# Four-chunk Strassen scheme of a sparse-attention and MLP kernel: DMA issues behind the exponentials, new shares of down steps, a pair's first block moved

## The chip, the core and the metric

The kernel runs on one core of one Trainium2 chip. The metric is the device time of one execution in microseconds (us), median of several runs. The program is written with a fixed schedule: the order in which the Python code issues instructions is the order in which each engine runs them. TensorE is PE in the rows, its weight loads PEld, VectorE DVE, ScalarE ACT, GpSimd POOL, SyncE SP; a q behind the name (ACTq, SPq) marks the engine's sequencer at work, as when it issues a DMA.

## The reference

Block-sparse attention over 4 x 8 heads of 768 x 64, then an MLP on its 3072 x 512 output.

```python
mask = np.abs(blk_i - blk_j) <= 1            # blocks of 32
mask |= (blk_i == 0) | (blk_j == 0) | (blk_i == 23) | (blk_j == 23)
for qb in range(24):
    for kb in sampled_blocks[qb]:            # three more key blocks
        mask[qb*32:(qb+1)*32, kb*32:(kb+1)*32] = True
scores = np.where(mask, scale * q @ k.T, -1e9)
attn = softmax(scores)
x = (attn @ v).transpose(0, 2, 1, 3).reshape(3072, 512)
h = x @ w_in                                 # 512 x 2048
g = h * (1.0 / (1.0 + np.exp(-1.702 * h)))
out = g @ w_out                              # 2048 x 512
```

## The kernel before

**The MLP.** The 3072 tokens are six chunks of 512, the 2048 hidden features sixteen slices of 128. A step m is one slice of one chunk: `up` makes h (12 matmuls of 128x512), `gate` makes g by a tanh on ACT and a product on DVE (`times`, L610 or L986), and `down` adds g times a slice of w_out to four output banks (12 matmuls). Every fp32 factor is split in a high and a low part, so a product is three matmuls. `gate_hi` casts g to ghi on ACT (L615), `gate_lo` subtracts on DVE (L623). `down` is two parts: 8 matmuls with ghi (L650, L652), then 4 with glo (L646).

**w_out.** Its rows stand in DRAM as `ws`; `stream` (L573) fetches the 256 KB of one slice into a tile `wst`, `split` casts the high part on ACT (L578) and subtracts the low part on DVE (L579) into one of three `wout` tiles. In the first chunk the weights are converted from 64-bit words instead (`weights`: L501, L516 on ACT, L540 to L551 and L509 on DVE).

**Attention.** An item is 64 query rows of all heads: `scores` (L343, 32 matmuls into banks 0 and 1), `least` (maximum on DVE, L360, and its negation nm, L362), four exponentials on ACT (L378), transposes of the exponentials (`turned`, L396, four to a bank, copied out by ACT, L402), `values` (L425, 64 matmuls), `normalise` (DVE, L441 to L451), and `turn` (L458, two transposes), whose result ACT and DVE split into x (L465, L466).

**The stages.** Chunks 0 and 1 run as 32 ticks (`tick`), with the attention items set among the quarters of the ticks by `plan`: an item begins every three quarters. Chunks 2 to 5 run in `last`: twice, eight calls of `pair(p)` do the up steps of two chunks by a seven-product Strassen scheme, in blocks of 6 matmuls (`half`, L970). A pair starts with block a11 x b11 into bank x, which ACT copies out (`snap`, L1001) before the block s2 x t2 is added to the same bank. One chunk of the two goes down within the pass, in `slot`s; the gates of the other are kept. Between the two passes stands `stretch`: the 16 down steps of the kept chunk (`drain`, a generator that yields after each matmul) run among the last 16 attention items. `go(k)` takes k of these 192 matmuls.

In `stretch`, item j is issued in this order: scores of item j, `least`, values of item j-2, transposes of item j-1, `go(DRAIN)`, exponentials of item j, `turn` of item j-2, first transposes of item j. A down step sets three lists of work for other engines, `hooks`: [0] casts, [1] subtractions, [2] the next `stream`, on ACT's queue. At the start of each down step `drain` calls `settle()`, which empties all three, so a `stream` that falls due in `go` stands ahead of the exponentials on ACT:

```python
least()
...
self.settle((1,))
go(DRAIN if g else 4)
finish(exps)
```

The tile into which a `stream` writes is that of the slice just split, so the DMA waits for the subtraction L579 on DVE. DMAs of SP and ACT also take eight completion semaphores in turn, and each waits for the one eight before it.

Of the kernel before, what the change touches and what calls it, by code (L numbers as in the profile page):

```python
# [27 lines left out]
NF = DF // P  # L28
# [3 lines left out]
CT = CU * UT  # L32
# [10 lines left out]
MAIN = (NC - TAIL) * NF  # L43
LATE = 2 * CU
NEXTQ = QT * NF - 4
STRIDE = 3
DRAIN = 10
SPARE = (7, 1, 2, 0)
DV = D + 1
VROW = H * DV  # L50
# [7 lines left out]
class Kernel:  # L58
# [640 lines left out]
    def plan(self):  # L699

        at = {}
        assert all(self.sparse(g) for g in self.behind + self.latter)
        starts = [(8 * k - 8 if k < CU else NEXTQ + STRIDE * (k - CU), g) for k, g in enumerate(self.behind)]
        starts.append((starts[-1][0] + STRIDE, None))
        put = lambda q, part, g: at.setdefault(q, []).append((part, g))
        for k, (q, g) in enumerate(starts):
            before = starts[k - 1][1] if k else None
            turn = q + (2 if k >= CU else 4)
            if g is not None:
                if q >= 0:  # L710
                    put(q, self.scores, g)
                if turn >= 0:
                    put(turn, self.transposes, g)
            if before is not None:
                assert q >= 0
                put(q, self.values, before)
                put(turn, self.turn, before)
        return at
# [9 lines left out]
    def tick(self, m):  # L728

        n0, n1, n2 = 0, 0, 0  # L730
# [4 lines left out]
        def run(n):  # L735
            for _ in range(n):
                next(self.conv, None)
# [17 lines left out]
        put_off, self.put_off = self.put_off, None  # L755
        self.up(m, range(2, 4))
        after = self.begin(QT * m + 2)
        soon = NF - 3 <= m < NF
        self.gate(m, lambda: (self.flush(), run(0 if soon else n1)))
        if soon:  # L760
            run(n1)
        finish(put_off)
        finish(after[:3])
        self.down(m - LAG, 0)
# [220 lines left out]
    def times(self, g, h):  # L985
        self.nc.vector.scalar_tensor_tensor(out=g, in0=g, scalar=1.0, in1=h, op0=ALU.add, op1=ALU.mult)  # L986

    def pair(self, p):

        nc = self.nc  # L990
        x, z, y = (self.bank[SPARE[n]] for n in (p % 2, 2, 3))
        a11, a12, a22 = self.block(2 * p + 1, 0), self.block(2 * p + 1, 1), self.block(2 * p, 1)
        s1, s2, s3, s4 = ([w[:, n] for w in self.sums] for n in range(4))
        b11, b21, b22, t1, t2, t3, t4 = self.right
        again = self.again
        m = MAIN + 2 * NF * again + 2 * p

        def snap(bank):
            s = self.store2[:, CT * (4 + self.nsnap % 4):CT * (5 + self.nsnap % 4)]
            self.nsnap += 1  # L1000
            nc.scalar.copy(out=s, in_=bank)  # L1001
            return s

        two = p or again
        self.half(x, a11, b11, True)
        p1 = snap(x)
        self.half(z, a12, b21, True)
        self.add(p1, p1, z)
        self.room_for(p)
        self.slot(m - 2 if two else m - 1, 0)  # L1010
        next(self.prep, None)
# [33 lines left out]
            self.mixed(p + 1)  # L1045
        if not again and p == 0:
            self.keep_sums(1)
        g = self.work.tile([P, CT], F32, name="g")
        self.tanh(g, u2)
        self.times(g, u2)  # L1050
# [2 lines left out]
            self.slot(m - 1, 1)  # L1053
        self.tanh(self.kept(2 * p), x)
        self.times(self.kept(2 * p), x)
        self.gate_hi(m + 1)
        self.gate_lo(m + 1)

    def kept(self, f):

# [54 lines left out]
    def drain(self, start, end):  # L1115

        for d in range(start, end):
            self.settle()
            if d + 1 >= start + 2:
                self.next_gate(d + 1)  # L1120
            for part in range(2):
                yield from self.products(d, part)
            self.split(d + 2, self.hooks)
            if d + 6 < end + 4:
                self.hooks[1].append(lambda d=d: self.hooks[2].append(
                    lambda: self.stream(d + 6, ("wst", "g")[(d + 6) // 2 % 2], self.nc.scalar)))

    def stretch(self):
# [5 lines left out]
        def go(k):  # L1134
            for _ in range(k):
                next(todo, None)

        items = self.latter
        self.hooks = [], [], []
        self.where = {"s": (0, 1), "t": (2, 2), "a": (7,)}  # L1140
        start, end = MAIN + NF - 2, MAIN + 2 * NF - 2
        todo = self.drain(start, end)
# [9 lines left out]
        self.settle()  # L1152
        self.room(1, tr, self.store2)
        self.klimit, self.vlimit = len(self.kent), len(self.vent)
        go(16)
        self.settle()
        prep = self.prepare_again()
        n = len(items)
        for j in range(n + 2):
            g, one, two = (items[k] if 0 <= k < n else None for k in (j, j - 1, j - 2))  # L1160
            exps = []
# [8 lines left out]
            if one:  # L1170
                self.turned(one, 1)()
            self.settle((1,))
            go(DRAIN if g else 4)
            finish(exps)
            if two:
                finish(self.turn(two))
# [6 lines left out]
            self.settle((0,))  # L1183
            if j in (11, 13, 14, 15, 16, 17):
                next(prep)
        for _ in todo:
            pass
        self.settle()
# [6 lines left out]
    def last(self):  # L1195
        self.gate_lo(MAIN - 1)
        self.gates, self.keep = {}, {}
        for again in range(2):
            self.again = again
            for p in range(NF // 2):  # L1200
                if not again and p == 5:
                    self.room(0, self.store1, self.store1[:, 8 * CT:])
                self.pair(p)
            if not again:
                self.stretch()
        end = NC * NF
# [121 lines left out]
    def run(self):  # L1328
# [30 lines left out]
        for m in range(MAIN):  # L1359
# [2 lines left out]
                    pass  # L1362
                self.third()
            self.tick(m)
            if m in (NF + 1, NF + 2, NF + 3, NF + 7, NF + 8, NF + 9, NF + 10):
                next(early_sums, None)
                next(early_sums, None)
            if m >= MAIN - 5:
# [68 lines left out]
```

## Time and profile before

| what | value |
|---|---|
| time, median of 3 runs | 737.93 us (736.52 to 740.36) |
| time of the profiled execution | 738.39 us |
| span of the profiled execution | 736.6 us |
| PE busy | 711.9 us, 97% of the span |
| DVE, ACT, POOL busy | 501.2, 414.1, 77.1 us |
| granted TensorE clock, mean | 0.999 |
| ticks with attention | about 72 to 326 us |
| first pass of pairs | about 327 to 446 us |
| stretch | about 446 to 562 us |
| second pass and last down steps | about 562 to 733 us |

An engine's row in the timeline gives the start, the length, the engine, the line, what was written from what, the count, and in brackets the idle time before it and what ended it. The end of a matmul is modelled: one of 128x512 is shown 0.39 us long, though the next begins sooner, so the idle time shown before a PE row is less than what its wait cost.

### The profile page before, as it was taken

The numbers are of one execution on the slowest core, as the hardware profiler recorded it, in microseconds if no ns is written. First come the engines' busy times: TensorE is split into PE (matmuls) and PEld (weight loads), VectorE is DVE, ScalarE is ACT, GpSimd is POOL, SyncE is SP. The second block draws the span as 40 slices with busy tenths as digits, with TensorE's granted clock in tenths as the row PEclk, the third lists the DMA queues.
The fourth block names the chain that finished last, engine by engine and source line by source line (L and its number), as shares of the span: only waits on it lengthen the run. The fifth ranks groups of instructions, "written<-read, shape, count | busy, mean of one in ns | idle before, by whom it ended". The sixth has DMA issues, their size and how long they took to land.

```text
span 736.6 us, 18799 instructions
## 1 busy us (share of the span) xinstructions
PE 711.9 (97%) x7506; PEld 555.7 (75%) x7506; DVE 501.2 (68%) x927; ACT 414.1 (56%) x804; POOL 77.1 (10%) x128
## 2 busy tenths in 40 slices
PE   7999999999999999999999999999998999999997
PEld 5666777886777767787888887666766788888886
DVE  5686989987656556578777666445668877766553
ACT  5776767775554644355455455555565555455542
POOL 3163101101111110003000010112120100000000
PEclk9999999999999999999999999999999999999999
DMA  8996887876687781329601527888862711101533
GB/s 351 410 412 217 261 275 239 290 248 222 212 266 225 245 276 38 95 77 281 206 28 43 160 66 239 259 271 258 269 199 70 260 42 28 44 29 43 141 104 85
DMA packets 62985, 137.86 MB, mean 187 GB/s; under 512 B 7409, under 2 KB 25586, under 8 KB 62898
## 3 DMA queue, kind: packets, MB, share of 16 engines
q1 hardware_dynamic: 44000, 76.39, 32.7%
q0 software_dynamic: 9504, 34.97, 14.2%
q10 hardware_dynamic: 9394, 25.30, 10.1%
q8 instruction: 59, 0.97, 0.5%
q14 instruction: 28, 0.23, 0.1%
HBM read 119.33 MB, written 17.30 MB: 185 GB/s over the span
## 4 chain that ended last, share of the span: by engine, by line
PE 74%; DMA 8%; DVE 7%; ACT 6%; issue 3%; SPq 2%; ACTq 1%; DVEq 0%
PE banks L970 19%; PE banks L650 9%; PE banks L646 9%; PE banks L652 9%; PE banks L343 5%; PE banks L396 5%; PE banks L425 5%; PE banks L595 4%; PE banks L597 3%; PE banks L596 3%; DMA tk<-in_kb_dram 2%; DMA raw<-in_moe_w_in_dram 2%; DMA vmid<-in_vm_dram 2%; DVE mx L360 1%; DVE wout L579 1%
## 5 line engine op out<-in xcount | busy, mean ns | idle before, releaser
L650 PE MATMUL banks<-wout,ghi 128*128 128x512 f32 x376 | 148.6, 395 | 0.0
L652 PE MATMUL banks<-wout,ghi 128*128 128x512 f32 x376 | 146.8, 390 | 1.5 <-DVE wout L509 1.5
L646 PE MATMUL banks<-wout,glo 128*128 128x512 f32 x376 | 105.2, 394 | 0.0
L652 PEld LDWEIGHTS banks<-wout,ghi 128*128 128x128 f32 x376 | 70.6, 188 | 16.2 <-DVE wout L509 2.2
L650 PEld LDWEIGHTS banks<-wout,ghi 128*128 128x128 f32 x376 | 70.6, 188 | 15.7 <-DVE ot L692 0.5
L646 PEld LDWEIGHTS banks<-wout,glo 128*128 128x128 f32 x376 | 69.4, 188 | 14.3
L579 DVE TENSOR_TENSOR wout<-wst,wout 128x512 fp32r<-128x512 f32 x80 | 55.1, 689 | 34.4 <-ACT wout L578 31.8
L1001 ACT COPY store<-banks 128x512 f32<-128x512 f32 x64 | 37.5, 586 | 67.7 <-PE banks L970 67.6
L360 DVE TENSOR_REDUCE mx<-banks 128x4 f32<-128x1024 f32 x44 | 53.7, 1221 | 25.9 <-PE banks L343 25.8
L378 ACT ACTIVATE ex<-banks,nm 128x256 f32<-128x256 f32 x112 | 43.9, 479 | 42.9 <-DVE rg L441 34.7
L615 ACT CAST ghi<-g 128x512 fp32r<-128x512 f32 x64 | 40.1, 626 | 28.3 <-DVE g L986 17.4
L578 ACT CAST wout<-wst 128x512 fp32r<-128x512 f32 x80 | 49.9, 623 | 9.5 <-DMA wst<-ws 7.3
L595 PE MATMUL banks<-x,win 128*128 128x512 f32 x128 | 53.1, 414 | 0.1
L402 ACT COPY pt<-banks 128x512 f32<-128x512 f32 x80 | 43.9, 594 | 12.5 <-PE banks L396 11.4
L596 PE MATMUL banks<-x,win 128*128 128x512 f32 x128 | 50.1, 391 | 0.0
L597 PE MATMUL banks<-x,win 128*128 128x512 f32 x128 | 50.1, 391 | 0.0
L970 PE MATMUL banks<-x,win 128*128 128x512 f32 x192 | 48.0, 391 | 1.0 <-DVE x L780 0.9
L970 PE MATMUL banks<-x,tr 128*128 128x512 f32 x192 | 47.5, 389 | 0.0
L283 POOL DMA_INDIRECT vown<-in_v_dram,vidx x28 | 27.0, 965 | 190.0 <-PE banks L425 181.2
L396 PEld LDWEIGHTS banks<-ident,ex 128*128 128x128 f32 x308 | 34.3, 140 | 15.8 <-ACT pt L402 5.5
L396 PE MATMUL banks<-ident,ex 128*128 128x128 f32 x308 | 42.4, 277 | 3.6 <-ACT pt L402 2.5
L623 DVE TENSOR_TENSOR glo<-g,ghi 128x512 fp32r<-128x512 f32 x64 | 44.0, 688 | 1.5
(158 smaller groups left out, 1334.2 us busy)
## 6 DMA issues: line engine op xcount, KB each, us to landing
wst<-ws SPq DMA_DIRECT2D x66, 256.0 KB
kg<-in_kb_dram SPq DMA_DIRECT2D x70, 128.0 KB
raw<-in_moe_w_in_dram ACTq DMA_DIRECT2D x16, 512.0 KB
raw<-in_moe_w_out_dram ACTq DMA_DIRECT2D x16, 512.0 KB
vown<-in_vd_dram SPq DMA_DIRECT2D x8, 780.0 KB
out_dram<-ot SPq DMA_DIRECT2D x40, 128.0 KB
ws<-a ACTq DMA_DIRECT2D x16, 256.0 KB
kg<-in_kb_dram SPq DMA_DIRECT2D x10, 384.0 KB
```

The costliest lines, as they stand in the source:

```text
L360: nc.vector.tensor_reduce(out=mx.rearrange("p (i h) -> p h i", h=2), in_=self.banks[:, at:at + 2, 0:2 * n].rearrange("p h (i s) -> p h i s ...
L396: self.nc.tensor.transpose(ps[:, slot], g["ex"][h][:, k * P:(k + 1) * P], self.ident)
L578: parts = [lambda: self.nc.scalar.copy(out=t[:, 0:DM], in_=w), lambda: self.nc.vector.tensor_tensor(out=t[:, DM:2 * DM], in0=w, in1=t[:, 0 ...
L579: lambda: self.nc.vector.tensor_tensor(out=t[:, DM:2 * DM], in0=w, in1=t[:, 0:DM].bitcast(F32), op=ALU.subtract)]
L595: nc.tensor.matmul(h, wih[:, k], hi[:, k], start=(k == 0), stop=False)
L596: nc.tensor.matmul(h, wih[:, k], lo[:, k], start=False, stop=False)
L597: nc.tensor.matmul(h, wil[:, k], hi[:, k], start=False, stop=(k == NCT - 1))
L623: self.nc.vector.tensor_tensor(out=glo, in0=g, in1=ghi.bitcast(F32), op=ALU.subtract)
L646: nc.tensor.matmul(o[n], glo[:, tk[n]], woh, start=False, stop=last)
L650: nc.tensor.matmul(o[n], ghi[:, tk[n]], woh, start=(f == 0), stop=False)
L652: nc.tensor.matmul(o[n], ghi[:, tk[n]], wol, start=False, stop=False)
L970: self.nc.tensor.matmul(bank, a[:, k], b[:, k], start=start and k + n == 0, stop=k == 1 and n == 2, skip_group_check=True)
```

## The change

- In `drain` the settling at the start of a step takes a list, `calm`. During the items it is (0, 1): the stream is no longer issued there, but by the `settle((2,))` that stands behind the exponentials, the turn and the transposes.
- Of the 192 matmuls of the stretch, 18 instead of 24 come before the first item; the items take 13, 11, and then 9 each instead of 10 each; the two closing rounds 8 each instead of 4; and 8 stand behind the loop, ahead of the second pass.
- `ahead(p)` does the first block and its `snap` of pair p. It is called in pair p-1, ahead of the tanh of the second gate; `gate_hi` and `gate_lo` of that gate go into the next pair, behind its second block.
- In `tick`, the last three steps of chunk 0 no longer put the gate's product ahead of the weight conversion.
- `plan` sets the values of the last item before the passes one quarter later, and its turn too.
- `weigh_first` (sums of w_in slices on DVE, L780) runs behind other ticks.

```diff
-DRAIN = 10
+DRAIN = 9
...
-        starts.append((starts[-1][0] + STRIDE, None))
+        starts.append((starts[-1][0] + STRIDE + 1, None))
...
-        soon = NF - 3 <= m < NF
-        self.gate(m, lambda: (self.flush(), run(0 if soon else n1)))
-        if soon:
-            run(n1)
+        self.gate(m, lambda: (self.flush(), run(n1)))
...
+    def ahead(self, p):
+
+        if p < NF // 2:
+            x = self.bank[SPARE[p % 2]]
+            self.half(x, self.block(2 * p + 1, 0), self.right[0], True)
+            self.p1 = self.snap(x)
...
-        self.half(x, a11, b11, True)
-        p1 = snap(x)
+        snap, p1 = self.snap, self.p1
         self.half(z, a12, b21, True)
         self.add(p1, p1, z)
+        if p:
+            self.gate_hi(m - 1)
+            self.gate_lo(m - 1)
...
+        self.ahead(p + 1)
         g = self.work.tile([P, CT], F32, name="g")
         self.tanh(g, u2)
...
-        self.gate_hi(m + 1)
-        self.gate_lo(m + 1)
...
-            self.settle()
+            self.settle(self.calm)
...
-        go(16)
+        go(10)
...
+        self.calm = 0, 1
...
-            go(DRAIN if g else 4)
+            go((13, 11)[j] if j < 2 else DRAIN if g else 8)
...
+        self.calm = 0, 1, 2
         for _ in todo:
...
-            if m in (NF + 1, NF + 2, NF + 3, NF + 7, NF + 8, NF + 9, NF + 10):
+            if m in (NF + 2, NF + 3, NF + 5, NF + 6, NF + 8, NF + 9, NF + 10):
```

ACT, in the middle of the stretch, one item before. The names: store and xk are transposed exponentials and the exponentials themselves, wst to wout the split of a slice, ws the rows in DRAM, x the item's result, keep the kept gates.

```order
L402 COPY store_5106<-banks 128x512
L578 CAST wout_133<-wst 128x512
L573 DMA wst<-ws_93 128x512
L378 ACTIVATE xk<-banks,nm 128x256 x4
L465 CAST x_1380<-banks 128x4x64
L402 COPY xk<-banks 128x512
L615 CAST ghi<-keep_5496 128x512
```

The same engine and place in the changed kernel:

```order
L402 COPY store_5106<-banks 128x512
L578 CAST wout_133<-wst 128x512
L378 ACTIVATE xk<-banks,nm 128x256 x4
L465 CAST x_1380<-banks 128x4x64
L402 COPY xk<-banks 128x512
L573 DMA wst<-ws_93 128x512
L615 CAST ghi<-keep_5496 128x512
```

The DMA moved from ahead of the four exponentials to behind the second copy, and stands now straight ahead of the cast of the next gate.

ACT, from the first to the second pair of the first pass, before. The names: tr takes the weight sums, g is a gate, store_5104 and keep the kept gates, store_5106 the snaps.

```order
L785 CAST tr<-store_5106 128x1024
L983 ACTIVATE g<-store_5106 128x512
L983 ACTIVATE store_5104<-banks 128x512
L615 CAST ghi<-g 128x512
L1001 COPY store_5106<-banks 128x512 x2
```

The same place in the changed kernel:

```order
L782 CAST tr<-store_5106 128x1024
L988 COPY store_5106<-banks 128x512
L980 ACTIVATE g<-store_5106 128x512
L980 ACTIVATE store_5104<-banks 128x512
L615 CAST ghi<-g 128x512
```

The first snap of the second pair moved ahead of the two tanh and of the cast.

PE, the last round of the stretch and the start of the second pass, before. The names: wout with ghi or glo a down step, ident with xk a turn, xhi or xlo with win the first block of the pass.

```order
L425 MATMUL banks<-store_5106 32x65 x8
L646 MATMUL banks<-wout_134,glo 128x512 x4
L458 MATMUL banks<-ident,xk 128x128 x2
L970 MATMUL banks<-xhi_3172,win_7984 128x512
L970 MATMUL banks<-xlo_3173,win_7984 128x512
```

The same place in the changed kernel, the second half of the round:

```order
L458 MATMUL banks<-ident,xk 128x128 x2
L650 MATMUL banks<-wout_134,ghi 128x512
L652 MATMUL banks<-wout_134,ghi 128x512
L650 MATMUL banks<-wout_134,ghi 128x512
L652 MATMUL banks<-wout_134,ghi 128x512
L646 MATMUL banks<-wout_134,glo 128x512 x4
L967 MATMUL banks<-xhi_3172,win_7959 128x512
L967 MATMUL banks<-xlo_3173,win_7959 128x512
```

Between the last turn and the first block of the second pass there stand now eight matmuls of a down step, where there were none.

## Rows read from the trace of the kernel before

**Rows 1.** Busy us by window: PE, PEld, DVE, ACT, POOL; clock, DMA share, GB/s.

```profile
20.00:40.00 20.00, 18.85 (x364) 13.28 (x366) 14.53 (x33) 16.04 (x32) 4.69 (x10) 1.00 1.02 410
360.00:380.00 20.00, 20.00 (x90) 16.55 (x89) 12.88 (x23) 9.88 (x17) 0.00 (x0) 1.00 0.14 43
500.00:520.00 20.00, 19.20 (x349) 13.53 (x348) 10.97 (x25) 11.82 (x27) 2.66 (x3) 1.00 0.88 284
```

**Rows 2.** PE's waits in the stretch, 446 to 563 us: total, times, longest.

```profile
PE banks L396 <- ACT xk L378: 5.2, 13, 0.8
PE banks L425 <- DVE xlo L466: 1.4, 2, 0.9
PE banks L970 <- DVE xlo L466: 0.9, 1, 0.9
PE banks L458 <- DVE xk L451: 0.2, 1, 0.2
```

**Rows 3.** Timeline of PE over two neighbouring items of the stretch.

```profile
485.61 0.66 PE L396 MATMUL banks<-ident,xk 128*128 128x128 f32 x4
...
488.61 0.60 PE L396 MATMUL banks<-ident,xk 128*128 128x128 f32 x4
489.14 1.09 PE L343 MATMUL banks<-tk 64*32 64x256 f32 x32
...
491.21 0.66 PE L396 MATMUL banks<-ident,xk 128*128 128x128 f32 x4
...
494.66 0.80 PE L396 MATMUL banks<-ident,xk 128*128 128x128 f32 x4 [0.29 <-ACT xk L378]
495.39 1.45 PE L343 MATMUL banks<-tk 64*32 64x256 f32 x32
```

**Rows 4.** Timeline of ACT and DVE over the same two items.

```profile
486.78 1.57 ACT L378 ACTIVATE xk<-banks,nm 128x256 f32<-128x256 f32 x4
...
491.60 0.17 DVE L362 TENSOR_SCALAR nm<-mx 128x4 f32<-128x4 f32 x1
...
492.38 0.62 ACT L578 CAST wout<-wst 128x512 fp32r<-128x512 f32 x1
...
493.04 0.69 DVE L579 TENSOR_TENSOR wout<-wst,wout 128x512 fp32r<-128x512 f32 x1 [0.53 <-ACT wout L578]
...
493.76 0.33 ACTq L573 DMA_DIRECT2D wst<-ws  x1
494.13 1.57 ACT L378 ACTIVATE xk<-banks,nm 128x256 f32<-128x256 f32 x4 [1.13 <-DVE wout L579]
```

**Rows 5.** Timeline of PE: the same transposes 13 items apart.

```profile
465.11 0.66 PE L396 MATMUL banks<-ident,xk 128*128 128x128 f32 x4
...
550.64 0.65 PE L396 MATMUL banks<-ident,xk 128*128 128x128 f32 x4
```

**Rows 6.** Timeline of PE: twelve matmuls of 128x512 without a wait.

```profile
326.75 2.88 PE L970 MATMUL banks<-x,win 128*128 128x512 f32 x12
```

**Rows 7.** Timeline of PE: four waits outside the stretch.

```profile
181.26 0.50 PE L652 MATMUL banks<-wout,ghi 128*128 128x512 f32 x1 [0.68 <-DVE wout L509]
...
210.78 1.38 PE L396 MATMUL banks<-ident,ex 128*128 128x128 f32 x8 [0.41 <-ACT ex L378]
...
298.12 0.24 PE L425 MATMUL banks<-vown,pt 128*32 128x65 f32 x1 [0.60 <-DVE x L466]
...
345.83 1.65 PE L970 MATMUL banks<-tr 128*128 128x512 f32 x6 [0.59 <-ACT store L1001]
```

**Rows 8.** Timeline of DVE and ACT: what those four waits waited for.

```profile
180.52 0.68 DVE L509 TENSOR_TENSOR wout<-a,wout 128x512 fp32r<-128x512 f32 x1
...
206.43 1.29 DVE L780 TENSOR_TENSOR ot<-win 128x512 f32<-128x512 f32 x2
...
345.20 0.58 ACT L1001 COPY store<-banks 128x512 f32<-128x512 f32 x1
```

**Rows 9.** Chain of work in 466 to 512 us: one landing of a block of keys.

```profile
475.01 6.46 DMA tk<-in_kb_dram
```

More of the change, by code (lines that the diff above doesn't have):

```diff
@@ L986, in times, with snap @@
         self.nc.vector.scalar_tensor_tensor(out=g, in0=g, scalar=1.0, in1=h, op0=ALU.add, op1=ALU.mult)
+    def snap(self, bank):
+        s = self.store2[:, CT * (4 + self.nsnap % 4):CT * (5 + self.nsnap % 4)]
+        self.nsnap += 1
+        self.nc.scalar.copy(out=s, in_=bank)
+        return s
+    def ahead(self, p):
[3 more added lines that the diff above has]
+            self.p1 = self.snap(x)
     def pair(self, p):
-        nc = self.nc
         x, z, y = (self.bank[SPARE[n]] for n in (p % 2, 2, 3))
-        a11, a12, a22 = self.block(2 * p + 1, 0), self.block(2 * p + 1, 1), self.block(2 * p, 1)
+        a12, a22 = self.block(2 * p + 1, 1), self.block(2 * p, 1)
         s1, s2, s3, s4 = ([w[:, n] for w in self.sums] for n in range(4))
@@ L996, in pair @@
         m = MAIN + 2 * NF * again + 2 * p
[L998 to L1002, printed above, removed]
         two = p or again
-        self.half(x, a11, b11, True)
-        p1 = snap(x)
+        snap, p1 = self.snap, self.p1
         self.half(z, a12, b21, True)
         self.add(p1, p1, z)
+        if p:
+            self.gate_hi(m - 1)
+            self.gate_lo(m - 1)
         self.room_for(p)
@@ L1138, in stretch @@
         items = self.latter
-        self.hooks = [], [], []
+        self.hooks, self.calm = ([], [], []), (0, 1, 2)
         self.where = {"s": (0, 1), "t": (2, 2), "a": (7,)}
@@ L1199, in last @@
             self.again = again
+            self.ahead(0)
             for p in range(NF // 2):
@@ L1203, in last @@
                 self.pair(p)
+            m = MAIN + 2 * NF * again + NF - 1
+            self.gate_hi(m)
+            self.gate_lo(m)
             if not again:
```

## The prediction

> **What bounds the kernel now.** I read the busy times by window first, then the waits of PE, then the timelines of PE, ACT and DVE around the waits. In the passes of pairs PE is busy for all of a 20 us window, at full clock; there nothing is to be gained [rows 1]. In the stretch it is not: 19.20 of 20, and the true loss is larger than that, because a matmul is shown 0.39 long although twelve of them take 2.88, so the next begins (2.88 - 0.39) / 11 = 0.226 later [rows 1, 6]. Each wait that is shown on PE therefore cost about 0.39 - 0.23 = 0.16 more than its idle time. The waits of the stretch name one cause above all: transposes that wait for the exponentials, 13 times [rows 2].
>
> Two neighbours show what an item costs with and without that wait. From the transposes at 485.61 to those at 491.21 are 5.60 us: the next transposes start right behind the turn, and the scores take 1.09. The neighbour's transposes wait, take 0.80 instead of 0.60, and its scores take 1.45, because they write the two banks that the exponentials still read [rows 3]. Over 13 items the mean is (550.64 - 465.11) / 13 = 6.58 us, so nearly every item is of the second kind [rows 5].
>
> Why the exponentials are late is seen on ACT. In the clean item nothing stands ahead of them and they start at 486.78, 1.17 after the item's transposes. In the other the negated maximum is ready at 491.77 and the cast L578 is done at 493.00, but the DMA of the next w_out slice stands ahead on the same engine; it waits for the subtraction L579, which ends at 493.73, and the exponentials start at 494.13 [rows 4]. So the DMA holds them for about 1.1 us (494.13 - 493.00).
>
> **The change in the stretch.** The DMA goes behind the exponentials. They then start when the cast lets them: it starts at 492.38, which is 1.17 after the transposes at 491.21, and follows the copy before it; an ACT operation that follows another starts about 0.5 after it (the clean pair shows this for the copy and the exponentials), so they start at about +1.7 and end 1.57 later, at +3.27 [rows 3, 4]. PE comes to the item's own first transposes at 488.61 - 485.61 = +3.00, with nine matmuls instead of ten at +2.77; two of the four exponentials, which these need, are out at about +2.6. So that wait goes. The next scores come at 489.14 - 485.61 - 0.23 = +3.30 against +3.27: just free. What is late next is thus the end of the exponentials, by some hundredths.
>
> The period with nine matmuls is then between 5.60 - 0.23 = 5.37 (clean) and 5.73 (if the scores stretch by the full 1.45 - 1.09 = 0.36). The +3.27 lies at the clean end, so I take a third of the way, 5.50. Each item does one matmul less, worth 0.23, which is done elsewhere. Gain per item: 6.58 - 5.50 - 0.23 = 0.85, for 13 items **11.05 us**; by the two ends 12.7 and 8.1. The two items before 465 wait in the same way; they get 13 and 11 matmuls as cover, but the first one's exponentials come behind two evictions of output on ACT: 2 x 0.85 less 0.1, **1.6**.
>
> The matmuls taken from the items go to the end, four more into each of the two closing rounds and eight behind the loop. The waits for L451 and, at the first block of the second pass, for L466 (0.2 and 0.9) are then covered by eight matmuls, 1.8 us: with 0.16 each they give **1.4**. The two waits of `values` on L466 (1.4 together) stay: between the turn and the values there is still no down step [rows 2].
>
> Of the step that is moved also its lane and its consumers count. On ACT the DMA now stands ahead of the cast of the next gate, L615. An item's operations on ACT (four exponentials 1.57, the rest at about 0.5 from start to start, the DMA 0.33) fill some 4.3 of 5.5, so a hold of up to 1.2 costs nothing. What can hold it: the subtraction has long ended by then, but the DMA eight before must have landed, often a block of keys, and one of these took 6.46 [rows 9]. On SP the requests of keys keep their order.
>
> The rows of w_out are asked for some 2 us later in an item. They are used four down steps on, 48 matmuls, by then over five items or 27 us at 5.5, against that landing of 6.46 [rows 9]; I put this at zero. The Trainium skill, "DMA: Bandwidth & Descriptors", section "Rules for kernel authors", advises to issue a DMA early and to wait late, which speaks against this edit; no row here shows a w_out slice coming late in the stretch. By that rule the sum would lose up to 2 us at each of the 14 issues; by the row's slack it loses nothing.
>
> **The change elsewhere.** The conversion (`tick`): PE waits at 181.26 for L509, which stands behind the gate's product on DVE; now it stands ahead of that product. 0.68 + 0.16 and a slow first matmul (0.50 for 0.39) make **0.9**; between 0 and 0.95. The weight sums: two adds of L780 (1.29 for both at 206.43) stand ahead of the maximum of an item that begins a tick, and the transposes wait 0.41 and stretch. There are two such waits, alike; the sums now avoid ticks whose successor begins with scores. 0.41 + 0.16 + some 0.23 of stretch, twice, **1.6**; between 1.1 and 1.8. `plan`: the values at 298.12 wait for the split of the turn before them; six matmuls of the up step (1.36) now stand between, **0.75**. The pair's first block: at 345.83 the block s2 x t2 waits until the snap of the same bank, begun at 345.20 behind two tanh and a cast, is done; the snap now goes first and is out some 2 us ahead. 0.59 + 0.16 + 0.1, **0.85**, and a small wait of the same kind in the second pass, **0.2** [rows 7, 8].
>
> In the other pairs PE has no waits, and the early snap puts the tanh of the second gate behind six matmuls, 1.36 us [rows 1, 6]. That gate is used in the next pair, some 40 matmuls or 9 us later; I put it at zero. If that cover were gone, each of 14 pairs could lose up to 1.4.
>
> **Sum.** 11.05 + 1.6 + 1.4 + 0.9 + 1.6 + 0.75 + 0.85 + 0.2 = 18.35. The profiled execution took 738.39 (span 736.6), 0.46 above the median of 737.93; the forecast is 738.39 - 18.35 = **720.0 us**.
>
> **The rivals.** *Feed.* With shorter items the same bytes are wanted in less time. DMA is at 0.88 and 284 GB/s in the stretch; the opening reached 1.02 and 410 [rows 1]. By the share alone items could go 1.02 / 0.88 = 1.16 times as fast, 5.67 instead of 6.58, which is near my 5.50, and queues grow before the end is reached. If landings, or the DMA on ACT that waits for one, stretch the items to 6.0, the gain is 0.35 x 13 = 4.6 instead of 11.05: **726.5 us**. For it speaks the landing of 6.46; against it that PE shows no wait for a DMA in the stretch.
>
> *The exponentials are held by something else.* If the DMA only fills a time in which they would wait anyway, the stretch gives nothing but its ends, and 738.39 - 7.3 = **731 us** remain. The clean item, and nm ready 2.4 before the start, speak against it [rows 3, 4].
>
> *ACT held ahead of the gate's cast: slower.* Where the DMA eight before is a late block of keys, ACT stands, and with it the cast, the next copies and the next exponentials. Ten of 13 items issue such a DMA. Beyond the 1.2 of idle time every us is one more per item; it eats all 18.35 at 1.2 + 1.84 = 3.0 us of hold. At 3.5, which needs a landing like the one of 6.46 asked for 3 us before, the time is 738.39 - 18.35 + 10 x 2.3 = **743 us**. Against it: most of the awaited requests are an item old by then.
>
> *Late rows of w_out: slower*, the skill's rule of above taken as it stands. Once the 27 us do not cover the landing, the cast L578 waits ahead of the exponentials, up to 2 us at 14 issues: 738.39 - 18.35 + 28 = **748 us**.
>
> **How the numbers follow.** Forecast 0.67 (its own range 717 to 723.5: the item's period at its two ends gives 718.3 and 723.0, the smaller terms add half a microsecond up and one down), feed 0.20, held by something else 0.06, held cast 0.04 and late rows 0.01; 0.02 are left for a time near 738 by cases unnamed. The range is 716.5 to 727: it takes in the feed case, and below the 0.46 between the profiled execution and the median. 0.5% is about what a measurement of this kernel tells from no change, 734.2 to 741.6: faster 0.92, same 0.03, slower 0.05.
>
> **What would show it.** Right: the items' transposes 5.4 to 5.6 us apart, L378 starting 0.5 after L578, no waits of PE on L378 but a few tenths, none at the four places outside, the two of 1.4 on L466 still there. Wrong: periods of 6 and more with ACT's DMA waiting for tk or store, L615 late, PE waiting for ghi or wout in the stretch, or new waits in the pairs.

## The result, and the profile after

The changed kernel takes 727.12 us (median of 4 runs, 725.71 to 728.53) against 738.63 of the kernel before beside it (736.52 to 740.36): ratio 0.9845, 95% interval 0.9812 to 0.9879. In a later group of runs (e12 below) it was 0.9862 (0.9817 to 0.9907). It is faster, as forecast, but by 11.5 us and not by 18.35; 727.12 lies just above the range, 716.5 to 727.0. The profiled execution took 727.03, with a span of 725.2 for 736.6 before.

The page of the changed kernel, its first part:

```profile
span 725.2 us, 18776 instructions
...
PE 705.5 (97%) x7506; PEld 555.8 (77%) x7506; DVE 501.8 (69%) x927; ACT 413.1 (57%) x804; POOL 75.8 (10%) x128
```

**Where the 11.4 us between the two traces lie.** I measured both from landmark to landmark on PE. "Stretch" is from the last matmul of the first pass's last block to the first block of the second pass.

| piece | forecast gain | before, us | after, us | gain |
|---|---|---|---|---|
| opening, to the first up step (code unchanged) | 0 | 71.75 | 69.39 | 2.36 |
| conversion, 14th to 17th up step | 0.9 | 24.47 | 24.76 | -0.29 |
| two waits of the weight sums and the wait of `plan` | 2.35 | 140.54 | 138.07 | 2.47 |
| first block of the second pair | 0.85 | 38.71 | 37.79 | 0.92 |
| rest of the first pass | 0 | 79.56 | 79.56 | 0 |
| stretch | 14.05 | 117.31 | 110.95 | 6.36 |
| second pass | 0.2 | 119.69 | 120.03 | -0.34 |

The opening is not the change's: over all traces of this case it takes 69.1 to 73.3, and the changed kernel itself showed 69.39 and 71.50. Without it the traces differ by 9.05 us, so it is in part luck that the time came as near to the range as it did. The small terms hold but for the conversion and the second pass; the stretch gave less than half.

PE's waits in the stretch of the changed kernel, 436 to 552 us (total, times, longest). They answer to [rows 2]:

```profile
PE banks L343 <- DMA store<-in_kb_dram: 3.1, 1, 3.1
PE banks L343 <- DMA tk<-in_q_dram: 1.6, 1, 1.6
PE banks L425 <- DVE xlo L466: 1.4, 2, 0.9
PE banks L396 <- issue: 0.5, 1, 0.5
PE banks L425 <- issue: 0.3, 1, 0.3
```

All 13 waits for the exponentials are gone, and so are the waits for L451 and for L466 ahead of the second pass; the two waits of the values, 1.4, stay as forecast. New are two waits for a DMA. "issue" stands for a wait that ended with nothing that the profile shows. The timeline of PE shows the item as forecast first, and ACT beside it, the same places as [rows 3, 4]:

```profile
485.67 0.66 PE L396 MATMUL banks<-ident,xk 128*128 128x128 f32 x4
...
488.47 0.60 PE L396 MATMUL banks<-ident,xk 128*128 128x128 f32 x4
489.00 1.09 PE L343 MATMUL banks<-tk 64*32 64x256 f32 x32
...
491.07 0.66 PE L396 MATMUL banks<-ident,xk 128*128 128x128 f32 x4
```

```profile
486.84 0.62 ACT L578 CAST wout<-wst 128x512 fp32r<-128x512 f32 x1
487.36 1.57 ACT L378 ACTIVATE xk<-banks,nm 128x256 f32<-128x256 f32 x4
...
489.16 0.33 ACTq L573 DMA_DIRECT2D wst<-ws  x1
489.58 0.62 ACT L615 CAST ghi<-keep 128x512 fp32r<-128x512 f32 x1
```

The period is 491.07 - 485.67 = 5.40, the exponentials start 0.52 after the cast, the DMA stands behind them and holds nothing. Then the stop, at the scores of the fifth item:

```profile
465.23 0.60 PE L396 MATMUL banks<-ident,xk 128*128 128x128 f32 x4
468.95 0.62 PE L343 MATMUL banks<-store 64*32 64x256 f32 x4 [3.12 <-DMA store<-in_kb_dram]
471.18 1.95 PE L343 MATMUL banks<-store 64*32 64x256 f32 x28 [1.61 <-DMA tk<-in_q_dram]
473.06 1.68 PE L425 MATMUL banks<-store,xk 128*32 128x65 f32 x64
474.68 0.66 PE L396 MATMUL banks<-ident,xk 128*128 128x128 f32 x4
```

From transposes to transposes 9.45 us; where nothing waits it is 2.61 (in the second experiment below, 465.49 to 468.10). So one place costs 6.84, of which the two waits shown are only 4.73. Most of the other 2.11 is PE's clock, in the table by windows (busy us of PE, PEld, DVE, ACT, POOL; then the granted clock, DMA share, GB/s):

```profile
465.00:470.00 5.00, 1.46 (x11) 0.74 (x9) 0.42 (x1) 1.16 (x3) 0.17 (x1) 1.00 0.91 314
470.00:475.00 5.00, 3.82 (x95) 2.58 (x96) 1.56 (x3) 0.00 (x0) 0.00 (x0) 0.66 0.72 238
```

PE works for 1.46 of 5 us, and in the next 5 the granted clock is 0.66 on the mean, so part of them runs at 1.2 GHz: 28 scores take 1.95, where 32 took 1.09. From these 28 to the next transposes (471.18 to 474.68) are 3.50 us; in the item above the same way with all 32 scores took 2.07 (489.00 to 491.07). At least 1.43 of the 2.11 is thus the lower clock.

**Why the keys are late.** SP's queue in the changed kernel:

```profile
445.05 6.45 SPq L270 DMA_DIRECT2D tk<-in_kb_dram  x6
451.54 0.43 SPq L281 DMA_DIRECT2D store<-in_vm_dram  x1
452.07 6.73 SPq L680 DMA_DIRECT2D out_dram<-ot  x8
458.90 0.53 SPq L234 DMA_DIRECT2D store<-in_q_dram  x1
...
461.20 6.32 SPq L270 DMA_DIRECT2D store<-in_kb_dram  x6
467.62 0.36 SPq L234 DMA_DIRECT2D tk<-in_q_dram  x1
```

SP is at its requests, and at the waits that belong to them, from 440.86 to 467.51 with hardly a pause. One pair's requests (queries, blocks, six blocks whose address comes from a register, about 1.13 each) take about 9 us, and eight stores of finished output stand ahead of those for the fifth item. The last of these six is asked for at 467.17, as the chain of work shows it, while PE is ready at 465.8:

```profile
467.17 0.34 SPq L270
```

The trace names the next queries at 471.18; those go into the other tile, so I read this as the last block landing at the same moment. In e11 and e13 below it is the keys that the trace names for the same 28 scores. The kernel before had the same row of requests, with no wait to show for it:

```profile
457.52 5.02 SPq L680 DMA_DIRECT2D out_dram<-ot  x8
...
465.07 6.71 SPq L270 DMA_DIRECT2D store<-in_kb_dram  x6
```

```profile
475.96 1.66 PE L343 MATMUL banks<-store 64*32 64x256 f32 x32
```

There the last block was asked for at 471.43 and the scores began at 475.96, 4.5 later. The block itself had been in for a while: from 474.2 to 475.2 the DMA view of that trace lists one queue alone, and it is not SP's but that of POOL's gather of values (L283, which began at 472.01):

```profile
q0 software_dynamic: 68, 0.28, 75.7%
```

So before, the landing took at most 2.8 us, and some 1.8 were to spare at this place. Measured from the start of the stretch (445.02 before, 439.58 after), three things used that up. PE reaches these scores 4.7 us sooner (at 26.2 instead of 30.9). The last block is asked for 1.2 later (at 27.6 instead of 26.4), because the eight stores hold SP for 6.73 instead of 5.02; 1.7 of the 6.73 is a wait for the landing of the middle rows (`in_vm`), and before there was no such wait. And the block takes 4.0 from request to use instead of at most 2.8. 4.7 - 1.8 + 1.2 + 1.2 = 5.3, which is the way from 465.8 to 471.18. So more was lost at this one place than had been gained up to it.

**The conversion** turned one wait into another. PE, DVE and ACT at the 14th up step of the changed kernel:

```profile
166.72 0.50 PE L595 MATMUL banks<-x,win 128*128 128x512 f32 x1 [1.62 <-DVE g L610]
```

```profile
163.72 0.43 DVE L540 TENSOR_SCALAR a<-a 128x512 int32<-128x512 int32 x1 [0.53 <-ACT a L501]
...
165.99 0.68 DVE L610 SCALAR_TENSOR_TENSOR g<-g,banks 128x512 f32<-128x512 f32 x1
```

```profile
163.02 0.67 ACT L501 ACTIVATE a<-raw 128x512 f32<-128x512 f32 x1 [0.88 <-DMA raw<-in_moe_w_out_dram]
```

In the last three steps of chunk 0 the product L610 reads the bank that the next up step writes. It now stands behind a conversion that waits for a raw slice, and PE with it.

### The profile page after: what moved, and what is told of

The parts are those of the page before. It is cut to its first block, busy times and chain, and to the rows that moved or that the text cites. A ratio compares the mean times of both kernels' runs of the same rounds, so it can differ in the third digit from the quotient of the medians.

```text
span 725.2 us, 18776 instructions
## 1 busy us (share of the span) xinstructions
PE 705.5 (97%) x7506; PEld 555.8 (77%) x7506; DVE 501.8 (69%) x927; ACT 413.1 (57%) x804; POOL 75.8 (10%) x128
## 4 chain that ended last, share of the span: by engine, by line
PE 49%; DVE 3%; ACT 2%; issue 2%; SPq 1%; DMA 0%; DVEq 0%; ACTq 0%
PE banks L967 19%; PE banks L650 7%; PE banks L652 7%; PE banks L646 7%; PE banks L343 3%; PE banks L425 2%; PE banks L396 2%; DVE store L777 1%; DMA tk<-in_q_dram 0%; PE banks L458 0%; ACT wout L578 0%; SPq L269 0%; SPq L270 0%; DVE mx L360 0%; DVE x L777 0%
## 5 line engine op out<-in xcount | busy, mean ns | idle before, releaser
L615 ACT CAST ghi<-g 128x512 fp32r<-128x512 f32 x64 | 39.9, 624 | 24.5 <-DVE g L983 12.5
L283 POOL DMA_INDIRECT vown<-in_v_dram,vidx x28 | 26.7, 955 | 188.9 <-PE banks L425 180.2
```

## The experiments

Theory: the items are freed as forecast, and SP's requests of keys take the gain back at the fifth item. Rivals: the bytes on the way are too many (landing), or the DMA of w_out was not what held the exponentials. Times are medians; "stretch" and "conversion" are pieces of each trace as in the table above.

| kernel | time, us | ratio to before | stretch | conversion |
|---|---|---|---|---|
| changed | 727.12 | 0.9845 [0.9812, 0.9879] | 110.95 | 24.76 |
| e1 stores on POOL | 722.77 | 0.9777 [0.9727, 0.9827] | 109.20 | 24.51 |
| e2 stores spread | 720.19 | 0.9760 [0.9716, 0.9805] | 103.86 | 25.23 |
| e3 stream back | 735.35 | 0.9963 [0.9935, 0.9991] | 119.30 | 22.85 |
| e4 old shares | 727.41 | 0.9845 [0.9799, 0.9891] | 111.85 | 24.49 |
| e5 stretch alone | 735.48 | 0.9917 [0.9892, 0.9942] | 111.55 | 25.20 |
| e6 no early block | 731.16, one run | - | 111.62 | 25.35 |
| e7 spread, one gate | 725.34 | 0.9788 [0.9729, 0.9847] | 103.94 | 25.65 |
| e8 and closing | 722.55 | 0.9744 [0.9703, 0.9785] | 104.22 | 25.31 |
| e9 spread, closing, first pass | 723.41 | 0.9772 [0.9725, 0.9819] | 102.95 | 23.76 |
| e10 spread again | 724.38 | 0.9794 [0.9743, 0.9845] | 105.44 | 25.85 |
| e11 half spread | 730.68, one run | - | 111.99 | 24.98 |
| e12 changed again | 730.89 | 0.9862 [0.9817, 0.9907] | 111.91 | 23.94 |
| e13 small stores | 726.90, one run | - | 112.19 | 23.55 |
| e14 stores on POOL again | 721.22, one run | - | 104.71 | 24.43 |

e1 to e4, e5 to e8, e9 to e12 and the last two ran together; before took 738.43, 741.55, 740.31 and 740.76 beside them, so times compare within a group, ratios and pieces across.

**e1: the stores from POOL.**

```diff
-                    nc.sync.dma_start(out=out[r0:r0 + UT], in_=src)
+                    queue.dma_start(out=out[r0:r0 + UT], in_=src)   # gpsimd in the first two items
```

> The changed kernel with one edit: the eight stores of a chunk's output that fall into the first two items of the stretch are issued from POOL and not from SP. In the changed kernel PE waits 3.12 and 1.61 us for keys at the scores of the fifth item (465.7 to 471.2). Theory 'SP's queue': SP issues without a pause from 440.86 to 467.51, and 6.73 of this are those eight stores, which stand ahead of the keys of the fifth item. Without them the last block is asked for at about 460.8 and lands some 3.6 later, at 464.4, ahead of 465.7: both waits go, 5.2 us with what they stretch, 727.1 becomes 721.9. Rival 'landing': the blocks come late because DMA has too many bytes under way (0.9 to 0.99 busy there); the stores bring the same bytes at the same time, the wait stays at 3 us or more and the time at 725 to 727.

The two waits at the fifth item went. Two others came in the profiled execution, the slowest of four (720.13 to 727.27): 1.4 for keys at the third item, and one of 3.5 at values later on that the trace puts to "issue". The stretch, 109.20, holds both. The stop at the fifth item is ended; what the bytes do at the third item is a smaller matter.

**e2: the stores spread.**

```diff
...                                          # the stores of the first two items are put into self.later
+            if j >= 2 and self.later:
+                self.later.pop(0)()          # one store, on SP
```

> The changed kernel with one edit: the same eight stores stay on SP, but one is issued in each of eight items, from the third item on. SP's queue: the wait at the fifth item goes (5.2 us); each later pair of items asks SP for two stores more, 1.2 us on top of 9.6 in a period of about 10.8 us, so a few tenths may come back at later items: 722 to 723.5. Landing: the bytes move from the first items to later ones, so by this theory too the wait shrinks, but not below 2 us, since the stores are 1 of some 7 MB in that stretch: 724 to 727.

Better than either expected. PE's waits of the whole stretch of this kernel, 436 to 558 us:

```profile
PE banks L426 <- DVE xlo L467: 1.4, 2, 0.9
PE banks L397 <- issue: 0.8, 1, 0.8
```

No wait for a key is left. The stretch takes 103.86, which is 13.45 less than before; the forecast was 14.05. In this trace the extra requests cost the later items nothing.

**e3: the stream back ahead of the exponentials.**

```diff
-            self.settle(self.calm)
+            self.settle()
```

> The changed kernel with the stream's DMA issued at the start of a down step again, ahead of the exponentials, the new shares kept. If this DMA holds the exponentials, items take 6.5 us again instead of 5.4 to 5.7 (the matmul taken from an item only makes the wait for L378 longer): some 0.85 for each of 11 items from the fifth on, 9.4, and about 1 for each of the first four, of which the wait for keys at the fifth then gives back as much: 727.1 + 9.4 = 736.5 us, and a wait for keys of about 1 us or none. If the exponentials were held by something else, the items stay at 5.4 to 5.8 and the time at 727 to 729.

As the theory has it, 735.35. Its waits in the same stretch:

```profile
PE banks L396 <- ACT xk L378: 7.3, 12, 1.2
PE banks L425 <- DVE xlo L466: 1.6, 2, 1.1
PE banks L343 <- DMA store<-in_kb_dram: 1.1, 1, 1.1
```

The exponentials are late again, and with the items that slow the keys cost only 1.1. So the DMA did hold the exponentials, and the stop at the keys is what fast items run into.

**e4: the old shares.**

```diff
-            go((13, 11)[j] if j < 2 else DRAIN if g else 8)   # DRAIN 9, go(10) ahead
+            go(DRAIN if g else 4)                             # DRAIN 10, go(16) ahead
```

> The changed kernel with the old shares: 24 matmuls ahead of the first item, 10 in each, 4 in the closing rounds and none behind the loop; the stream stays behind the exponentials. PE then reaches the scores of the fifth item some 0.9 us later (6 matmuls more ahead, 4 fewer in the first two, 2 more in the next two), so by the theory of SP's queue the wait for keys is 4.3 instead of 5.2. Later items take 5.60 to 5.9, and the waits for L451 and L466 at the end come back, 1.4 us. In all 727.1 - 0.9 + 1.4 = 727.6 us, within 1.5: the shares alone bring little while the keys are late. If the shares had been what freed the items, periods go to 6 and more and the time to 731 or above.

727.41, close to the 727.6 expected, though with a wait of 5.3 at the fifth item where 4.3 was expected; the waits at the end are back. Periods were 5.60 to 5.63 (transposes at 482.40, 488.03, 493.63). The stretch, 111.85, is 0.9 longer than in the first trace of the changed kernel and as long as in its second (111.91, e12). So nearly all of the gain is the stream's place, and what the shares are worth beside the stop these runs don't tell.

**e5: the stretch's two edits on the kernel before.** The diff is the lines of `drain` and `stretch` in the change.

> The kernel before with the two edits in the stretch alone: the stream behind the exponentials and the new shares; conversion, weight sums, planner and first blocks as before. From the last block of the first pass to the first of the second the kernel before takes 117.3 us, the changed one 110.95. If the stretch decides alone, it takes 110 to 112 here as well, with the wait for keys of about 5 us at the fifth item, and the time is that of before less 6.4: 732 us. If the gain of the changed kernel came from elsewhere, 736 to 738. Beside it: the opening up to the first up step took 71.75 before and 69.4 in every changed kernel so far, though its code is the same; if that is chance it may be either here, if it hangs on the program as a whole it is 71.7.

735.48 against 741.55, 6.07 less; the stretch took 111.55 with the stop in it. The opening took 72.0 here, and 71.8 to 73.3 in the changed kernels of the same group, against 69.1 to 69.4 in the group of e1 to e4: it goes with the group of runs and not with the program.

**e6: without the early first block.** The diff is `ahead` and its calls, taken out.

> The changed kernel without the early first block of a pair (first block, snap and the gate's halves as before). Theory: only the wait at the second pair's block comes back (0.92 at about 341 us), and in the second pass one of 0.2 to 0.5, while the waits of the changed kernel at 569.2 and 570.0 (0.55 and 0.28, for the copies of output) go. So a difference of +0.9 in the first pass, -0.3 to +0.3 in the second: 727.7 us. Rival: the other pairs feel it too, some tenths in each of 14, 729 or above.

By pieces: the first block of the second pair 38.80 instead of 37.79 (+1.0), the rest of the first pass 79.56, the second pass 119.56 instead of 120.03 (-0.5). The other pairs show nothing, as forecast. The single time of 731.16 was 2.4 longer in the opening, so it decides nothing.

**e7: one gate ahead of the conversion.**

```diff
-        self.gate(m, lambda: (self.flush(), run(n1)))
+        soon = m == NF - 3
+        self.gate(m, lambda: (self.flush(), run(0 if soon else n1)))
+        if soon:
+            run(n1)
```

> The kernel with the spread stores (720.2 us), and in the third step from the end of chunk 0 alone the gate's product goes ahead of the conversion again. The changed kernel waits 1.78 at 166.7 for that product, which stands behind a conversion that waited for the landing of a raw slice. From that up step (the 14th) to the 17th PE needs 22.85 without any wait; before took 24.47, the changed kernel 24.76, the spread one 25.23. Theory: with the product ahead, PE no longer waits for the raw slice there: 23.3 to 24.0, and the time falls by about 1 to 719.2. Rival: the conversion as a whole is late with its raw slices, and the wait only moves to the next down step: 24.4 to 25.3 and 720.2 as before.

The rival was right. The wait for the product went, and PE waited 2.0 for a cast of w_out (L517) and 0.9 for its low part instead: 25.65. The conversion as a whole takes 22.85 to 25.85 over all traces, with the old order (24.47, 25.20) as with the new. It goes with ACT's waits for landings: in e3, whose code is the changed kernel's up to the stretch, its waits at L501 came to 8.9 us between 140 and 176 us and the conversion took 22.85; in the changed kernel they came to 10.5 and it took 24.76. A term of 0.9 can't be read from one pair of such traces.

**e8 and e9: the closing rounds.**

```diff
+            if n - 1 <= j <= n:
+                go(4)                        # behind the transposes, and behind the turn
```

> As the one before, and in the closing rounds of the stretch the down steps stand where PE waits: four matmuls behind the last item's transposes and four behind the next turn, taken from the 24 that stood elsewhere in the closing. The waits of the values for L466 (0.65 and 1.09 in the changed kernel) go, and with them 1.4 to 1.7 us: 717.7 us, the stretch 102.3. Rival: with fewer matmuls ahead of the turns these wait for the division L451 instead, 0.3 to 0.8 each, and 718.5 to 719.5 remain.

> The spread stores; in the closing rounds four matmuls behind the last item's transposes and four behind the next turn, with 5 and 6 ahead of the two last turns; and the early first block in the first pass alone, the second pass as in the kernel before. Theory: the three gains are of different places and add up. Against the spread kernel on the same chip: 1.2 to 1.7 less in the closing (two waits for L466), 0.45 less in the second pass (120.0 becomes 119.6), 1.6 to 2.1 in all. Rival: the waits at the end come back at L451 or at the copies of the output, 0.5 or less in all, which 5 rounds do not tell from nothing.

In both the waits of the values for L466 (1.4) went, and for the division came one of 0.4 in e8 and two of 0.7 together in e9. With 0.16 for each wait as in the prediction this is 1.2 and 0.7 us. In e8 two stops put to "issue" (1.0 and 1.2) hid it. e9's second pass took 119.90, not 119.6, so the 0.45 was not got. Neither differs from e7 or e10 by more than the intervals: the gain is seen in the waits of the traces and not in the times.

> The kernel with the spread stores again, now beside the changed kernel on one chip. By the stretches of the earlier traces (103.9 against 110.95) it is 7.1 us faster than the changed kernel; if part of the 6.9 between 727.1 and 720.2 was the chip's, 4 to 6.

> The changed kernel itself, beside the two others on one chip: the stretch takes 111 with the waits for keys at the fifth item, as in its first trace; the up steps 14 to 16 take anything from 22.9 to 25.4, as the raw slices land.

**e10 and e12** (no edit against e2 and the changed kernel): 724.38 and 730.89 on one chip, 6.5 us apart, and stretches of 105.44 and 111.91. So nearly the whole difference between e2 and the changed kernel is the stop. e12 shows it again, with waits of 3.2 and 1.6. By the means they are 5.0 apart, because two of e10's six executions took 729.8 and 730.2, at a granted clock of 0.995, where the execution that was traced had 0.999 and the two traces of the changed kernel 0.996. No trace of these two was kept; they may have had a stop of their own, so the spread stores need not end it in every execution.

**e11: four stores stay, four are spread.**

```diff
+            for n, ot in ots[:2]:
+                stores(n, ot)                # as before
-            for n, ot in ots:
+            for n, ot in ots[2:]:            # spread
...
```

> The spread kernel, but four of the eight stores stay where the changed kernel has them, ahead of the fifth item's keys, and four are spread. A dose: in the changed kernel the first four take 2.42 of SP's time and the other four 4.31 with their wait. Theory of SP's queue: the wait at the fifth item (5.26 with what it stretches) shrinks by what SP is spared, 4.3, to about 1 us. Rival, bytes under way: it shrinks by half, to 2.6.

Both fell: the stop stayed, 111.99. PE at the fifth item:

```profile
468.41 0.62 PE L344 MATMUL banks<-store 64*32 64x256 f32 x4
473.18 1.95 PE L344 MATMUL banks<-store 64*32 64x256 f32 x28 [4.15 <-DMA store<-in_kb_dram]
```

SP was spared the four stores, but then stood 2.0 us at a request whose turn of the eight semaphores was that of the middle rows (`in_vm`), issued eight before at 454.15. The last block was asked for at 467.34 and used at 473.18: 5.8 us instead of 4.0. That left open whether requests or bytes decide.

**e13 and e14: requests without bytes, bytes without requests.**

```diff
+                        nc.sync.dma_start(out=out[r0:r0 + 1], in_=src[0:1])       # old place
+                        q[0].dma_start(out=out[r0 + 1:r0 + UT], in_=src[1:UT])    # spread
...
```

The diff is e13's; e14 has the edit of e1.

> The spread kernel, but of each of the eight stores the first row alone (2 KB of 128) is stored where the changed kernel has the whole store, on SP ahead of the fifth item's keys; the other 63 rows follow one store an item. So SP has the eight requests there again, and nearly none of their bytes. If the requests of keys are late because SP is held (the requests themselves 0.55 each, and the wait for the completion eight requests before), the stop at the fifth item is back: 4 to 5.3 us of waits and a stretch of 110.5 to 112. If it is the bytes ahead of them, the stop is under 1 us and the stretch 104 to 105.5.

> The stores on POOL once more: the bytes are there in the first items, without SP's requests. In the first trace of this the fifth item's scores did not wait; the third's waited 1.4 for keys and a later item 3.7 for something the trace does not name. If the bytes were the cause, the fifth item waits 2 us or more in this trace; by SP's queue it does not, and the stretch takes 104 to 106 unless the 3.7 comes again.

PE's waits for a DMA in the stretch, first e13, then e14:

```profile
PE banks L344 <- DMA store<-in_kb_dram: 5.3, 1, 5.3
```

```profile
PE banks L344 <- DMA tk<-in_kb_dram: 1.0, 1, 1.0
```

Eight requests of 2 KB bring the stop back (112.19); the whole bytes from POOL do not (104.71, and 1.0 at the third item). So the stores delay the keys of the fifth item by their requests on SP and not by their bytes. Each of the two is a single execution, but the other traces of changed kernels with fast items sort the same way: with four or eight such requests ahead of the keys the stop is there (changed, e4, e5, e6, e11, e12), without them it is not (e1, e2, e7 to e10). The Trainium skill, "DMA: Bandwidth & Descriptors", section "Rules for kernel authors", says that spreading DMAs over the issuing engines brings no bandwidth and only saves issue time. The traces agree on the issue time: 6.7 us of it counted here. They hold no test of the bandwidth.

What stays open is the size of the stop. In e11 and e13 the last block was asked for earlier after the row of requests began (23.8 and 25.3 us after 443.53 and 439.56, for 26.3 in the changed kernel), yet it took 5.8 us to use and the stop was as long. With the 2.8 of the kernel before, the waits would have been 1.1 instead of 4.15 in e11 and 2.3 instead of 5.3 in e13 (an estimate: 467.34 + 2.8 and 464.81 + 2.8, less the 469.03 and 465.31 at which the waits begin). So much of these two stops is a slow landing. PE's row in e13:

```profile
470.58 1.95 PE L344 MATMUL banks<-store 64*32 64x256 f32 x28 [5.27 <-DMA store<-in_kb_dram]
```

The traces show what else was under way, POOL's gather of values, in the changed kernel:

```profile
462.70 0.94 POOL L283 DMA_INDIRECT store<-in_v_dram,vidx  x1 [27.71 <-PE banks L425]
```

It begins 22.6 to 24.7 us into the stretch in all fourteen traces with fast items. In the seven without the stop the last block is asked for 19.7 to 21.9 us into the stretch, ahead of the gather; in the seven with it at 25.1 to 28.3, behind it. From that request to the use of the block the gather's queue moved 0.53 MB in the changed kernel, 0.81 in e13 and 1.02 in e11. So the rival "landing" may still hold a part, with the gather's bytes in place of the stores'. That is argued and not shown: no run moves the gather. Nor do the runs tell what the waits named "issue" are; they come in every stretch with fast items, 0.2 to 1.2 us each, and once 3.5 (e1).

## Why the prediction was right, and where it was wrong

**The mechanism of the stretch was right.** The DMA held the exponentials (e3), behind them the items run at 5.37 to 5.59 where nothing else waits (5.50 forecast), and without the stop the stretch gains 13.45 (e2) or 11.87 (e10) of the 14.05. Over eleven periods of e2 the mean is (530.06 - 468.10) / 11 = 5.63, the waits named "issue" among it.

**The step that failed** is the sentence that the requests of keys keep their order on SP. They do; but a queue that is never empty doesn't get faster because its order stays. I counted DMA share and GB/s for the feed and not SP's own time, although the trace of the kernel before has it: the last block of the fifth item was asked for 4.5 us ahead of its use and was in some 1.8 ahead. The gain of four items, with the 1.4 of the six matmuls taken from ahead of the first, came to 4.7 and ran past that; and request and landing themselves came later by 1.2 each. The term of 14.05 for the stretch measured 6.36, and 6.84 of the difference of 7.7 is this one stop.

**The rival "feed"** named 726.5, nearly the result, and the shape was wrong: it had all items at 6.0, by share of bytes or landings. In truth one item stands and the others run free. What comes late there is a request, and the landing behind it is slower too, so in part it is the rival's landing after all. That its time came near the result is luck. The argument against it, that PE showed no wait for a DMA, was worth little: where no wait is shown, the margin isn't shown either.

**The clock** was left out: this stop cost 4.7 in waits and 2.1 more, at least 1.4 of it at the lower clock.

**The conversion**, 0.9 forecast, gave -0.29. The step that failed is taking the wait at 181.26 for the cost of an order; the raw slices were late, and the other order passes their lateness on elsewhere (e7). My lower bound there was 0 and should have been negative.

**The small terms:** sums and `plan` 2.47 for 2.35, first block 0.92 for 0.85, end of the stretch as forecast (e4 brings its waits back). The second pass lost 0.34 where I had 0.2 of gain: its second slot now waits for a copy of output on ACT, 0.39 as shown and 0.55 in effect,

```profile
569.17 0.50 PE L650 MATMUL banks<-wout,ghi 128*128 128x512 f32 x1 [0.39 <-ACT ot L690]
```

and e6, without the early block, has no such wait. The zero for the other pairs held (79.56 in all traces).

**The slower rivals.** In the changed kernel no DMA held the cast of the next gate: in the item shown the DMA L573 and the cast L615 follow each other within 0.42, and ACT's waits in the stretch name no DMA. ACT shows no wait for a row of w_out in the stretch either. The advice of the Trainium skill to issue a DMA early ("DMA: Bandwidth & Descriptors", section "Rules for kernel authors"), which I had weighed against this edit, so changed nothing here; it bears on the keys, which were issued late. In the spread kernels the rival of the held cast does show: the DMA on ACT waited for landings of keys, 1.4 us in all in e2 and 3.6 in e8 and in e10 (2.9 the longest), but no wait of PE names it.

## What to carry to other kernels

Before a stretch is made faster, follow back the request of each block that it consumes: request, landing, use. The distance from landing to use is how much sooner the consumer may come, and an idle time of zero says nothing about it. Here the margin shrank besides, as request and landing came later once other transfers met them. Count the time of the issuing queue like that of an engine: if it issues without a pause, what stands ahead in it (here eight stores that nobody waits for) decides, and one store an item instead of eight at once gave back 6.5 us on the same chip.

## What the runs showed of the hardware

- Eight requests of 2 KB hold SP for 4.74 us, eight of 128 KB for 6.73, each with the waits among them (2.3 and 1.7 for completions; 5.02 in the kernel before, where none was for a completion). A block whose address comes from a register takes SP 1.13 us a request: six of them took 5.96 to 5.98 where no wait stood among them, (5.97 - 0.33) / 5.
- The completion semaphores taken in turn can take back what a shorter queue saves: in e11 SP stood 2.0 us for the landing of a transfer asked for eight requests before.
- The last block of keys took at most 2.8 us to land in the kernel before, where POOL's gather began behind its request, and 4.0 and 5.8 from request to use where the gather was under way (changed kernel; e11 and e13).
- After a stop in which PE worked for 1.46 of 5 us the granted clock fell to a mean of 0.66 in the next 5, and the stop cost 6.84 us instead of the 4.73 that the waits show, at least 1.43 of it by the lower clock.
